# Interleaving VectorE's expert and gate products, and inverting attention's softmax sums in a compact layout

## The chip, the core and the metric

The kernel runs on one core of a Trainium2 chip. Its time is the device time of one execution in microseconds. Several runs are taken; the median of three is 2377.94 us (2376.03 to 2380.96). One further execution was profiled, and all durations of single instructions come from it.

The core has engines that each work through a queue of their own: PE (TensorE, matmuls), VectorE (DVE in the profile), ScalarE (ACT), GpSimd (POOL) and SyncE (SP, which here only issues DMAs). They wait for each other by semaphores.

## The reference

A layer norm feeds two branches, and the result is `x + A(xn) + B(xn)`, for 2048 tokens of width 512.

```python
# A: attention, 32 heads of width 16, one shared k and v
scores = jnp.einsum("bhqd,bkd->bhqk", q, k) * (Dh ** -0.5)
p = _softmax(scores, axis=-1)
o = jnp.einsum("bhqk,bkd->bhqd", p, v)
...
# B: 4096 experts by product keys, 32 heads, 2 experts of each head
s1 = jnp.einsum("nhd,ed->nhe", q1, k1)
s2 = jnp.einsum("nhd,ed->nhe", q2, k2)
...
g = _softmax(top_s, axis=-1)
ue = u[top_e]
ve = v[top_e]
act = _gelu(jnp.einsum("nd,nhkd->nhk", xf, ue))
out = jnp.einsum("nhk,nhk,nhkd->nd", g, act, ve)
```

So every token picks 64 experts: for each it takes the dot of its own row with the expert's row of `u`, puts a gelu and a gate on it, and adds that multiple of the expert's row of `v`.

## The kernel before

The tokens stand in four groups of 512. A start part computes the layer norm, k, v and q, and stores what is needed later in DRAM. Then one loop in hand-written order (`manual_schedule`: each engine runs its instructions in the order of the code) carries four kinds of work:

**Attention.** `att_steps` is one step of 256 and handles two of a unit's 16 key chunks; a unit is four heads of 512 query rows, 32 units in all. `scores` (L311) makes two score tiles per chunk on PE, and ScalarE takes their exp (L314) into a probability tile `pt`, of which there are five. `pv` (L325) multiplies the four tiles of the step before with v; v has columns of ones beside it, so that the sums of the softmax come out as sixteen equal rows below each head's output. After the last chunk `unit_tail` copies the result to `e` (L333), and eight DMAs on SP take it apart into `ot` (outputs) and `rsb` (sums, still sixteen equal rows). Two units make a pair; 20 steps after a pair's start `pair_tail` inverts `rsb` (L349) and multiplies (L351) into `on`. `block_out` multiplies four pairs with wo (L360) and adds the experts' part, through one tile `fin`.

**Expert scores.** A generator, `score_thread`, is advanced a fixed amount in each step, at its end (`fill`, `run_scores`). It makes the key scores on PE (L452) for chunks of four heads, and VectorE finds the best two of each (L462, L464); `batch` turns them into expert numbers `idx` and gates `gg`, ten buffers each. `SEQ` is the order of the chunks: group 0, four chunks of group 1, group 2 and its dense stage, the rest of group 1, group 3 and its dense stage.

**Gathered experts (groups 0 and 1).** The work is 512 slots; a slot is one expert of 128 tokens. `gather` (L732, GpSimd) fetches the rows of u and v into one of nine tiles. `dot` (L744) multiplies the u half with the token's row, into a junk tile of which there is one, and sums up; after four dots L748 and L750 make the argument of the gelu's tanh, which `tanh` (L755) takes on ScalarE. `add` (L766, L767 before the first of four, then L772) adds the weighted v half to the accumulator. A slot's gather can start when the add nine slots before is done.

**Dense experts (groups 2 and 3).** `dense` first forms all gates by one-hot products on VectorE (L611 to L614) and PE (L628). Then, for 32 blocks of 128 experts, PE makes the dots (L675), ScalarE their squares (L694), VectorE two products out of PSUM (L695 for `g`, L696 for `y`), ScalarE the tanh of `y` (L704), and VectorE three more products (`gate`, L699 to L701), the last of which reads what the two others wrote. PE multiplies by v (L655) and VectorE adds (L658). GpSimd splits the raw rows for the matmuls (L589).

The order on VectorE within a step is set by the main loop:

```python
            if d < half * 3 // 4:
                pos += 2.4 if dense_on[0] else 1.65
            ...
            dots(int(pos + 0.001))
            def mid():
                tanhs(before)
                run(ON_ACT)
                run(BEHIND)
                adds(4)
                gathers(4)
```

`pos` is the slot to which the dots have to come; after three quarters of the steps the rest is spread evenly. So a turn of VectorE is: the step's dots, then what `behind` put aside (the gate products), then up to four adds, and, at the end of the step, what the generator brings. `tanhs` and `ON_ACT` put the two kinds of tanh into ScalarE's queue, behind the step's first two exps. `store` puts DMAs aside until the start of the next step (`run(STORES)`).

Of the kernel before, what the change touches and what calls it, by code (L numbers as in the profile page):

```python
# [22 lines left out]
P = 128  # L23
S = 2048
D = 512
# [17 lines left out]
NIDX = 10  # L43
# [10 lines left out]
def tile_kernel(ctx, tc, x, wq, wkv, wo, wqT, kT, uv, ub, vb, out):  # L54
# [21 lines left out]
    d_m = dram.tile([2, H, S], F32, name="dm")  # L76
    d_part = [dram.tile([P, D], F32, name=f"dpart{t}") for t in range(NT)]
# [107 lines left out]
    def project_kv(g):  # L185
# [17 lines left out]
        sq = big.tile([16, 512], BF16, name="ksq", tag="junk", bufs=1)  # L203
# [9 lines left out]
    def project_q(g, wqs):  # L213
        pq = xtile("pqs")
        for r in range(KC):
            p = stile("pq")[:, 0, :]
            n = 0
            for k in range(KC):
                for a, b in TERMS:
                    nc.tensor.matmul(p, wqs[k][:, a, r * P:(r + 1) * P], XT[g][k][:, b, :],  # L220
                                     start=n == 0, stop=n == 11)
                    n += 1
            q = [start.tile([P, 512], F32R, name="qt", tag="qt", bufs=4) for _ in range(2)]
            nc.scalar.copy(q[0], p)
            nc.vector.tensor_tensor(out=q[1], in0=p, in1=q[0], op=OP.subtract)
            sq = big.tile([P, 512], BF16, name="qsq", tag="junk", bufs=1)
# [12 lines left out]
    def guard():  # L239

        mm = small.tile([P, 2], F32, name="mm")
# [5 lines left out]
        m2 = small.tile([1, 2], F32, name="m2")  # L247
        nc.vector.reduce_max(m2, p[:1, :2 * P].rearrange("p (a n) -> p a n", a=2), axis=AX.X)
        pr = small.tile([1, 1], F32, name="prd")
        nc.vector.tensor_mul(pr, m2[:, 0:1], m2[:, 1:2])  # L250
        fl = small.tile([1, 1], I32, name="flag")
# [5 lines left out]
    def true_maxima():  # L257
        ptile = lambda dt, shape: late[0].tile(list(shape), dt, name="mx", tag="pt", bufs=5)
# [48 lines left out]
    def scores(u, kc, i):  # L307
        p = stile("sc")
        for b in range(2):
            o = 64 * b  # L310
            nc.tensor.matmul(p[:, b, :], kaug[o:o + 64, kc * P:(kc + 1) * P], QA[u][o:o + 64, i, :],  # L311
                             start=True, stop=True)
        pt = late[0].tile([P, 2, 512], F32, name="pt", tag="pt", bufs=5)
        nc.scalar.activation(pt, p, AF.Exp, scale=SCALE)  # L314
        PT[u, kc, i] = pt
# [14 lines left out]
    def unit_tail(u):  # L330
# [4 lines left out]
        def spread():  # L335
            if half == 0:
                ot = late[0].tile([P, 512], F32, name="ot", tag="ot", bufs=1)
                rs = late[0].tile([P, 512], F32, name="rsb", tag="rsb", bufs=1)
                OT[pp], RB[pp] = ot, rs
            for j in range(4):  # L340
                o = slice(64 * half + 16 * j, 64 * half + 16 * j + 16)
                nc.sync.dma_start(OT[pp][o, :], e[32 * j:32 * j + 16, :])
                nc.sync.dma_start(RB[pp][o, :], e[32 * j + 16:32 * j + 32, :])

        store(spread)

    def pair_tail(pp):
        rs = RB.pop(pp)
        nc.vector.reciprocal(rs, rs)  # L349
        on = late[0].tile([P, 512], F32, name="on", tag="on", bufs=4)  # L350
        nc.vector.tensor_mul(on, OT.pop(pp), rs)  # L351
        ON[pp] = on

    DONE_A, DONE_B = {}, {}

    def block_out(qb, j):
# [5 lines left out]
        fin = late[0].tile([P, D], F32, name="fin", tag="fin", bufs=1)  # L362
        if t in DONE_B:
            nc.sync.dma_start(fin, d_part[t])
# [57 lines left out]
    def wp_read(n, ks=range(KC)):  # L422
        for k in ks:
# [4 lines left out]
    SEQ = ([(0, c) for c in range(NC)] + [(1, c) for c in range(4)] + [(2, c) for c in range(NC)]  # L428
           + [(1, c) for c in range(4, NC)] + [(3, c) for c in range(NC)])
# [127 lines left out]
    def dense(DG, after):  # L557

        flush()
        df1, df2, dgt = DT[:3]  # L560
        formed = [0]
# [107 lines left out]
        for b in range(NB):  # L669
# [24 lines left out]
            nc.scalar.activation(y, p, AF.Square, scale=C_CUB ** 0.5)  # L694
            stt(g, g, 1.0 / GS, p, op0=OP.mult, op1=OP.mult)  # L695
            stt(y, y, C_IN, p, op0=OP.add, op1=OP.mult)  # L696

            def gate(y=y, g=g, wd=wd):
                stt(wd[:, 0, :], y, 1.0, g, op0=OP.add, op1=OP.mult)  # L699
                stt(y, y, 1.0, g, op0=OP.add, op1=OP.mult)  # L700
                nc.vector.tensor_tensor(out=wd[:, 1, :], in0=y, in1=wd[:, 0, :], op=OP.subtract)  # L701
# [3 lines left out]
            behind(gate)  # L705
            held.append((wd, vs))
# [16 lines left out]
    UV, WT, ACTS, TH = {}, {}, {}, {}  # L723
# [13 lines left out]
    def dot(m):  # L737
# [5 lines left out]
        junk = big.tile([P, D], BF16, name="junk", tag="junk", bufs=1)  # L743
        nc.vector.tensor_tensor_reduce(junk, UV[m][:, :D], XN[TPH * ph + ti], scale=1.0, scalar=0.0,  # L744
                                       op0=OP.mult, op1=OP.add, accum_out=a[:, i:i + 1])
        if i == SB - 1:
# [4 lines left out]
            TH[n] = y  # L751

# [5 lines left out]
    def add(m):  # L758
        ph, c, ti, s = slots[m]
        n, i = divmod(m, SB)  # L760
        if i == 0:
            a, th = ACTS.pop(n), TH.pop(n)
            s0 = s
            ga = small.tile([P, SB], F32, name="ga", bufs=3)
            w = small.tile([P, SB], F32, name="w", bufs=3)
            nc.vector.tensor_mul(ga, a, G[ph, c, ti][:, s0:s0 + SB])  # L766
# [90 lines left out]
    def att_steps(d, mid, fill):  # L857
# [22 lines left out]
        if i >= 40 and (i - 40) % 32 == 0 and i - 40 < STEPS:  # L880
            pair_tail((i - 40) // 32)
# [53 lines left out]
    with tc.manual_schedule(engines={E_.PE, E_.Activation, E_.DVE, E_.Pool, E_.SP}):  # L935
# [3 lines left out]
        for d in range(half + 24):  # L939

            if d < half * 3 // 4:
                pos += 2.4 if dense_on[0] else 1.65
            else:
                pos += max(0.0, NSL - pos) / max(half - 4 - d, 1)
            before = d_next[0]
            dots(int(pos + 0.001))

            def mid():
                tanhs(before)
                run(ON_ACT)  # L950
                run(BEHIND)
                adds(4)
# [49 lines left out]
```

## Time and profile before

| | |
|---|---|
| median of three runs | 2377.94 us |
| the profiled execution, and the span of its instructions | 2381.03 us, 2379.1 us |
| granted clock of PE, mean | 0.909 |
| DMA: bytes moved, mean rate | 491.99 MB, 207 GB/s |
| ScalarE's exps (L314), busy | 1016.9 us |
| slot dots and adds (L744, L772), busy | 410.3 and 385.0 us |

A row of the groups view reads: line, engine, operation, output tile<-inputs, shapes, count, then busy time and mean of one in ns, then the engine's idle time just before these instructions, and what ended it. A row of the timeline reads: start and duration in us, engine, line, operation, tiles, count of merged instructions, and in brackets the idle time before and its releaser. A row of the stages view reads: stretch, its length, busy time and count of PE, PEld (weight loads), DVE, ACT and POOL, then the granted clock, the DMA engines' share and GB/s; limited to one line of the code, it has only the engines that the line uses. A row of the waits view reads: who waited, for whom, us in total, times, longest.

### The profile page before, as it was taken

What the parts mean: (1) busy time and instruction counts of PE and PEld (TensorE: products, weight loads), DVE (VectorE), ACT (ScalarE), POOL (GpSimd) and SP (SyncE); (2) the same over time, 40 slices, a digit from 0 to 9 for tenths busy, and PEclk for the clock granted to TensorE, in tenths of its full rate; (3) what the DMA queues carried; (4) which work ended last, traced back from release to release, by engine and by line L of the source; (5) the groups of instructions that cost most, each with busy time, mean ns of one, the idle gap of its engine ahead of it and who ended that gap; (6) DMA issues with size and microseconds to landing.
All of it is one profiled execution on the core that took longest, in us unless ns stands there. A gap on an engine that the chain in (4) does not pass through costs nothing.

```text
span 2379.1 us, 35223 instructions
## 1 busy us (share of the span) xinstructions
PE 2019.6 (85%) x10990; PEld 1064.9 (45%) x10990; DVE 1928.2 (81%) x6683; ACT 1274.4 (54%) x1702; POOL 767.9 (32%) x670
## 2 busy tenths in 40 slices
PE   5859899999987788888888899997777888888886
PEld 3534444545444344444444455544343444444442
DVE  5648788999997577999988689999786879899882
ACT  2335455555555565656565455554565555565652
POOL 2012222222231224544544322222124344445430
PEclk9979999999998779999899999999777898999897
DMA  5776666776564566766756876755467666666561
GB/s 196 259 251 205 220 220 244 263 247 224 189 206 127 156 170 208 232 190 203 233 190 220 286 254 224 258 188 173 123 178 227 207 204 197 206 219 213 195 200 65
DMA packets 236097, 491.99 MB, mean 207 GB/s; under 512 B 90736, under 2 KB 90736, under 8 KB 235904
## 3 DMA queue, kind: packets, MB, share of 16 engines
q0 software_dynamic: 73728, 268.47, 33.9%
q1 hardware_dynamic: 159504, 218.17, 28.6%
q10 hardware_dynamic: 2672, 3.05, 0.4%
q8 instruction: 88, 1.44, 0.2%
q14 instruction: 105, 0.86, 0.1%
HBM read 422.18 MB, written 58.20 MB: 202 GB/s over the span
## 4 chain that ended last, share of the span: by engine, by line
DVE 28%; PE 27%; issue 21%; POOL 9%; DMA 6%; ACT 2%; SPq 1%; POOLq 0%; DVEq 0%; ACTq 0%
PE pv L325 8%; PE psc L452 6%; DVE xa L772 6%; PE sc L311 6%; POOL g L732 5%; DVE i L464 5%; DVE junk L744 4%; POOL wk L589 4%; DVE m L462 3%; DMA g<-in_uv_dram,idx 2%; PE pwo L360 2%; ACT pt L314 2%; PE pout L655 2%; PE pact L675 1%; DVE rsb L349 1%
## 5 line engine op out<-in xcount | busy, mean ns | idle before, releaser
L314 ACT ACTIVATE pt<-sc 128x1024 f32<-128x1024 f32 x1024 | 1016.9, 1024 | 584.2 <-PE sc L311 474.8
L732 POOL DMA_INDIRECT g<-in_uv_dram,idx x512 | 584.9, 1142 | 1506.2 <-DVE xa L772 1295.0
L325 PE MATMUL pv<-pt,vaug 128*32 128x512 f32 x4096 | 540.8, 649 | 0.0
L311 PE MATMUL sc<-qa,kaug 64*128 64x512 f32 x2048 | 441.6, 492 | 57.2 <-ACT pt L314 44.5
L744 DVE CUSTOM_DVE_ANT_0 junk<-g,xa 128x512 bf16<-128x512 f32 x512 | 410.3, 801 | 56.3 <-DMA g<-in_uv_dram,idx 47.3
L772 DVE SCALAR_TENSOR_TENSOR xa<-g,w,xa 128x512 f32<-128x512 f32 x512 | 385.0, 752 | 18.5 <-DVE w L767 0.6
L452 PE MATMUL psc<-wk,xt 128*128 128x512 f32 x1536 | 386.6, 402 | 15.1 <-DMA xt<-dxt 4.1
L311 PEld LDWEIGHTS sc<-qa,kaug 64*128 64x128 f32 x2048 | 182.5, 194 | 442.8 <-ACT pt L314 292.9
L452 PEld LDWEIGHTS psc<-wk,xt 128*128 128x128 f32 x1536 | 280.8, 189 | 101.3 <-issue 21.4
L655 PE MATMUL pout<-wk,wd 128*128 128x512 f32 x768 | 224.1, 443 | 87.6 <-DVE gy L696 71.6
L675 PE MATMUL pact<-xt,wk 128*128 128x512 f32 x768 | 215.9, 430 | 33.3 <-DVE da L658 18.5
L325 PEld LDWEIGHTS pv<-pt,vaug 128*32 128x32 f32 x4096 | 113.1, 115 | 277.0 <-issue 275.5
L655 PEld LDWEIGHTS pout<-wk,wd 128*128 128x128 f32 x768 | 158.2, 213 | 139.7 <-DVE gy L696 82.9
L464 DVE FIND_INDEX8 i<-m,psc 128x8 uint32<-128x64 f32 x1024 | 206.3, 220 | 0.0
L675 PEld LDWEIGHTS pact<-xt,wk 128*128 128x128 f32 x768 | 152.1, 205 | 84.2 <-DVE da L658 22.6
L589 POOL TENSOR_TENSOR wk<-rw,wk 128x512 fp32r<-128x512 f32 x128 | 166.3, 1328 | 40.4 <-ACT wk L588 32.8
L462 DVE MAX8 m<-psc 128x8 f32<-128x64 f32 x1024 | 146.0, 213 | 40.1 <-PE psc L452 40.1
L628 PE MATMUL pg<-oh 128*128 128x32 f16 x1024 | 75.5, 247 | 56.8 <-DVE oh L614 56.8
L704 ACT ACTIVATE gy<-gy 128x512 f32<-128x512 f32 x64 | 40.3, 631 | 132.7 <-DVE gy L696 132.0
L628 PEld LDWEIGHTS <-oh 128*128 128x128 f16 x1024 | 70.9, 161 | 66.7 <-DVE oh L611 44.5
L588 ACT CAST wk<-rw 128x512 fp32r<-128x512 f32 x128 | 74.0, 629 | 35.7 <-PE pout L655 21.0
L658 DVE TENSOR_TENSOR da<-da,pout 128x512 f32<-128x512 f32 x128 | 82.2, 679 | 5.4 <-PE pout L655 5.4
(144 smaller groups left out, 1455.9 us busy)
## 6 DMA issues: line engine op xcount, KB each, us to landing
wk<-dw SPq DMA_DIRECT2D x96, 512.0 KB
wqt<-in_wqT_dram SPq DMA_DIRECT2D x32, 512.0 KB
dw<-wk SPq DMA_DIRECT2D x32, 512.0 KB
rw<-in_ub_dram SPq DMA_DIRECT2D x64, 256.0 KB
rw<-in_vb_dram SPq DMA_DIRECT2D x64, 256.0 KB
dg<-gst SPq DMA_DIRECT2D x32, 512.0 KB
gy<-dg SPq DMA_DIRECT2D x64, 256.0 KB
g<-in_uv_dram,idx POOLq DMA_INDIRECT x512
```

What stands on the lines that cost most here:

```text
L311: nc.tensor.matmul(p[:, b, :], kaug[o:o + 64, kc * P:(kc + 1) * P], QA[u][o:o + 64, i, :], start=True, stop=True)
L314: nc.scalar.activation(pt, p, AF.Exp, scale=SCALE)
L325: nc.tensor.matmul(PV[u][32 * j:32 * j + 32, :], vaug[:, kc, :], pt[:, b, :], start=kc == 0, stop=kc == 15)
L452: nc.tensor.matmul(p, XT[g][k][:, a, j * P:(j + 1) * P], WC[n_][k][:, bb, :], start=n == 0, stop=n == 11)
L462: nc.vector.max(m8[:, jb, s, :], p[:, s * E:(s + 1) * E])
L464: nc.vector.max_index(i8[:, jb, s, :], m8[:, jb, s, :], p[:, s * E:(s + 1) * E])
L589: nc.gpsimd.tensor_tensor(out=w[:, 1, :], in0=rw[:, i, :], in1=w[:, 0, :], op=OP.subtract)
L655: nc.tensor.matmul(p, wd[:, a, j * P:(j + 1) * P], vs[:, c, :], start=n == 0, stop=n == 5)
L675: nc.tensor.matmul(p, us[:, a, k * P:(k + 1) * P], XT[DG][k][:, c, :], start=n == 0, stop=n == 11)
L732: nc.gpsimd.indirect_dma_start(out=gt, out_offset=None, in_=uv, in_offset=bass.IndirectOffsetOnAxis(ap=IDX[ph, c, ti][:, s:s + 1], axis=0))
L744: nc.vector.tensor_tensor_reduce(junk, UV[m][:, :D], XN[TPH * ph + ti], scale=1.0, scalar=0.0, op0=OP.mult, op1=OP.add, accum_out=a[:, i:i ...
L772: nc.vector.scalar_tensor_tensor(acc, v, w[:, i:i + 1], acc, op0=OP.mult, op1=OP.add)
```

## The change

On VectorE a turn now alternates: one set-aside product group, one dot, one add, and again, until all three are used up. The gate is split in two groups: the two products, and the difference that reads them. The two products out of PSUM change places, `y` first. A dot writes its products over the u row that it has read, and the junk tile is gone (the start part's squares get tiles of their own). The product of dot and gate, `ga`, moves from `add` to `dot`. A step does as many adds as it has dots, two at least, while attention runs.

The sums of a pair (not of the last) go by another way: one row of each head is written to DRAM (`d_sum`), read back as 128 x 32, inverted there, written to DRAM (`d_inv`) and read back spread over sixteen rows each, into a tile that shares its place with `e`. This takes 4 to 14 key chunks after the pair's end, in five steps of code. There are six probability tiles in place of five, nine index buffers in place of ten. Slots per step are 1.75 in the score stages, 1.2 in the one-hot stages and 2.4 in the dense ones. `SEQ` takes two chunks of group 1 ahead of group 2 instead of four. At the end four `fin` tiles are loaded in one go into probability tiles.

```diff
@@
-NIDX = 10
+NIDX = 9
@@ project_kv, and likewise project_q
-        sq = big.tile([16, 512], BF16, name="ksq", tag="junk", bufs=1)
+        sq = start.tile([16, 512], BF16, name="ksq", tag="sq", bufs=2)
@@ scores
-        pt = late[0].tile([P, 2, 512], F32, name="pt", tag="pt", bufs=5)
+        pt = late[0].tile([P, 2, 512], F32, name="pt", tag="pt", bufs=6)
@@ unit_tail
+            if pp < 15:
+                nc.sync.dma_start(d_sum[pp, 4 * half:4 * half + 4, :],
+                                  e.rearrange("(j r) n -> j r n", r=32)[:, 16, :])
             for j in range(4):
                 o = slice(64 * half + 16 * j, 64 * half + 16 * j + 16)
+                if pp == 15:
+                    nc.sync.dma_start(RB[pp][o, :], e[32 * j + 16:32 * j + 32, :])
                 nc.sync.dma_start(OT[pp][o, :], e[32 * j:32 * j + 16, :])
-                nc.sync.dma_start(RB[pp][o, :], e[32 * j + 16:32 * j + 32, :])
...
+    def pair_load(pp):
+        rc = small.tile([P, 32], F32, name="rc", bufs=1)
+        nc.sync.dma_start(rc, d_sum[pp].rearrange("h n -> (h n)").rearrange("(p n) -> p n", n=32))
+        RC[pp] = rc
+
+    def pair_invert(pp):
+        rc = RC.pop(pp)
+        nc.vector.reciprocal(rc, rc)
+        store(lambda: nc.sync.dma_start(d_inv[pp].rearrange("h n -> (h n)").rearrange("(p n) -> p n", n=32), rc))
+
+    def pair_spread(pp):
+        rs = late[0].tile([P, 512], F32, name="rsb", tag="e", bufs=1)
+        RB[pp] = rs
+        nc.sync.dma_start(rs, d_inv[pp].rearrange("h n -> h () n").to_broadcast([8, 16, 512]))
 
     def pair_tail(pp):
         rs = RB.pop(pp)
-        nc.vector.reciprocal(rs, rs)
-        on = late[0].tile([P, 512], F32, name="on", tag="on", bufs=4)
-        nc.vector.tensor_mul(on, OT.pop(pp), rs)
+        ot = OT.pop(pp)
+        if pp == 15:
+            nc.vector.reciprocal(rs, rs)
+            on = ot
+        else:
+            on = late[0].tile([P, 512], F32, name="on", tag="on", bufs=4)
+        nc.vector.tensor_mul(on, ot, rs)
         ON[pp] = on
...
+    def load_fin():
+        for j in range(4):
+            if 12 + j in DONE_B:
+                pt = late[0].tile([P, 2, 512], F32, name="pt", tag="pt", bufs=6)
+                FIN[j] = pt[:, 0, :]
+                nc.sync.dma_start(FIN[j], d_part[12 + j])
@@
-    SEQ = ([(0, c) for c in range(NC)] + [(1, c) for c in range(4)] + [(2, c) for c in range(NC)]
-           + [(1, c) for c in range(4, NC)] + [(3, c) for c in range(NC)])
+    SEQ = ([(0, c) for c in range(NC)] + [(1, c) for c in range(2)] + [(2, c) for c in range(NC)]
+           + [(1, c) for c in range(2, NC)] + [(3, c) for c in range(NC)])
@@ dense
         df1, df2, dgt = DT[:3]
+        dense_on[0] = 2
...
             nc.scalar.activation(y, p, AF.Square, scale=C_CUB ** 0.5)
+            stt(y, y, C_IN, p, op0=OP.add, op1=OP.mult)
             stt(g, g, 1.0 / GS, p, op0=OP.mult, op1=OP.mult)
-            stt(y, y, C_IN, p, op0=OP.add, op1=OP.mult)
 
             def gate(y=y, g=g, wd=wd):
                 stt(wd[:, 0, :], y, 1.0, g, op0=OP.add, op1=OP.mult)
                 stt(y, y, 1.0, g, op0=OP.add, op1=OP.mult)
+
+            def rest(y=y, wd=wd):
                 nc.vector.tensor_tensor(out=wd[:, 1, :], in0=y, in1=wd[:, 0, :], op=OP.subtract)
                 formed[0] += 1
 
             on_act(lambda y=y: nc.scalar.activation(y, y, AF.Tanh))
             behind(gate)
+            behind(rest)
@@ dot
-        junk = big.tile([P, D], BF16, name="junk", tag="junk", bufs=1)
-        nc.vector.tensor_tensor_reduce(junk, UV[m][:, :D], XN[TPH * ph + ti], scale=1.0, scalar=0.0,
+        u = UV[m][:, :D]
+        nc.vector.tensor_tensor_reduce(u, u, XN[TPH * ph + ti], scale=1.0, scalar=0.0,
                                        op0=OP.mult, op1=OP.add, accum_out=a[:, i:i + 1])
...
+            ga = small.tile([P, SB], F32, name="ga", bufs=4)
+            nc.vector.tensor_mul(ga, a, G[ph, c, ti][:, s0:s0 + SB])
+            GA[n] = ga
@@ att_steps
-        if i >= 40 and (i - 40) % 32 == 0 and i - 40 < STEPS:
-            pair_tail((i - 40) // 32)
+        pp, r = divmod(i, 32)
+        if pp and pp < 16:
+            if r == 4:
+                pair_load(pp - 1)
+            if r == 6:
+                pair_invert(pp - 1)
+            if r == 10:
+                pair_spread(pp - 1)
+            if r == 14:
+                pair_tail(pp - 1)
+        if i == STEPS + 4:
+            load_fin()
+            pair_tail(15)
@@ the main loop
-                pos += 2.4 if dense_on[0] else 1.65
+                pos += (1.75, 2.4, 1.2)[dense_on[0]]
             else:
                 pos += max(0.0, NSL - pos) / max(half - 4 - d, 1)
-            before = d_next[0]
-            dots(int(pos + 0.001))
 
             def mid():
-                tanhs(before)
+
+                tanhs(d_next[0])
                 run(ON_ACT)
-                run(BEHIND)
-                adds(4)
+                rest = BEHIND[:]
+                BEHIND.clear()
+                todo = min(int(pos + 0.001), NSL) - d_next[0]
+                sums = min(a_ready[0] - a_next[0], max(todo, 2) if d < half else 4)
+                while rest or todo > 0 or sums > 0:
+                    if rest:
+                        rest.pop(0)()
+                    if todo > 0:
+                        dots(d_next[0] + 1)
+                        todo -= 1
+                    if sums > 0:
+                        adds(1)
+                        sums -= 1
                 gathers(4)
```

More of the change, by code (lines that the diff above doesn't have):

```diff
@@ L225, in project_q @@
             nc.vector.tensor_tensor(out=q[1], in0=p, in1=q[0], op=OP.subtract)
-            sq = big.tile([P, 512], BF16, name="qsq", tag="junk", bufs=1)
+            sq = start.tile([P, 512], BF16, name="qsq", tag="sq", bufs=2)
             nc.scalar.activation(sq, p, AF.Square)
@@ L361, in block_out @@
                              start=k == 0, stop=k == KC - 1)
-        fin = late[0].tile([P, D], F32, name="fin", tag="fin", bufs=1)
+        if qb == 3 and j in FIN:
+            fin = FIN[j]
+        else:
+            fin = late[0].tile([P, D], F32, name="fin", tag="fin", bufs=1)
         if t in DONE_B:
-            nc.sync.dma_start(fin, d_part[t])
+            if j not in FIN:
+                nc.sync.dma_start(fin, d_part[t])
             nc.vector.tensor_add(fin, fin, p)
```

28 lines of the change are left out of this document (16 added, 12 removed).

## The prediction

> **What bounds the kernel now.** First the page's busy shares, then the engines by stage. The stage bounds are mine: expert scores of groups 0 and 1 (160 to 713 us), one-hot gates (to 898), dense experts (to 1345), scores (to 1657), one-hot (to 1816), dense (to 2303), end.
>
> ```profile
> PE 2019.6 (85%) x10990; PEld 1064.9 (45%) x10990; DVE 1928.2 (81%) x6683; ACT 1274.4 (54%) x1702; POOL 767.9 (32%) x670
> ```
> ```profile
> 160.00:713.00 553.00, 510.36 (x2780) 263.10 (x2780) 475.05 (x2708) 295.80 (x356) 126.81 (x113) 0.96 0.66 226
> 713.00:898.00 185.00, 144.86 (x1043) 72.10 (x1044) 124.27 (x251) 104.35 (x163) 43.71 (x35) 0.78 0.55 154
> 898.00:1345.00 447.00, 378.31 (x1931) 205.95 (x1931) 396.59 (x700) 263.88 (x355) 210.80 (x178) 0.92 0.66 215
> 1345.00:1657.00 312.00, 294.98 (x1600) 157.47 (x1598) 280.32 (x1673) 167.78 (x198) 78.35 (x70) 0.99 0.65 225
> 1657.00:1816.00 159.00, 118.28 (x934) 60.23 (x934) 121.60 (x270) 91.69 (x150) 43.55 (x35) 0.75 0.64 175
> 1816.00:2303.00 487.00, 414.08 (x2044) 221.60 (x2044) 418.20 (x752) 276.55 (x371) 227.78 (x191) 0.91 0.63 203
> ```
>
> Columns: length, then PE, PEld, DVE, ACT, POOL busy, PE clock. In the score stages PE is busy 92 and 95%: PE sets the pace, VectorE (86 and 90%) close behind. In the dense stages VectorE leads (89 and 86%) over PE (85%). In the one-hot stages nobody is above 78%: a serial ring of VectorE, PE and ScalarE.
>
> An attention step is eight score matmuls, sixteen pv and some fill. Their counts by stage give the steps: 552/8 = 69, 160/8 = 20, 328/8 = 41, 136/8 = 17.
>
> ```profile
> 160.00:713.00 553.00, 115.12 (x552) 47.78 (x552) 0.96 0.66 226
> 713.00:898.00 185.00, 36.01 (x160) 15.03 (x160) 0.78 0.55 154
> 1345.00:1657.00 312.00, 68.37 (x328) 28.24 (x328) 0.99 0.65 225
> 1657.00:1816.00 159.00, 31.88 (x136) 13.04 (x136) 0.75 0.64 175
> ```
>
> One PE-paced step, in the timeline:
>
> ```profile
> 401.05 0.73 PE L311 MATMUL sc<-qa,kaug 64*128 64x512 f32 x4
> ...
> 402.88 1.02 ACT L314 ACTIVATE pt<-sc 128x1024 f32<-128x1024 f32 x1 [0.20 <-PE pv L325]
> 403.57 0.88 PE L311 MATMUL sc<-qa,kaug 64*128 64x512 f32 x4
> 403.95 0.19 PEld L311 LDWEIGHTS sc<-qa,kaug 64*128 64x128 f32 x2 [0.20 <-ACT pt L314]
> ...
> 408.01 0.73 PE L311 MATMUL sc<-qa,kaug 64*128 64x512 f32 x4
> ```
>
> 408.01 - 401.05 = 6.96 us is the floor of a step. The second exp waits 0.20 us for a probability buffer, and the second score group then takes 0.88 instead of 0.73 us.
>
> **The change part by part.**
>
> *Six probability buffers.* The wait for pv goes, and with it up to 0.88 - 0.73 = 0.15 us of a PE-paced step, nothing of others. 69 + 41 steps x 0.15 = 16.5; a few are not PE-paced: 15 us at most, 10 for the first stage and 5 for the second. Late next is the exp pair itself.
>
> *Dots in place, woven adds.* VectorE in the dense stage:
>
> ```profile
> 1011.60 0.68 DVE L744 CUSTOM_DVE_ANT_0 junk<-g,xa 128x512 bf16<-128x512 f32 x1
> ...
> 1012.32 0.69 DVE L744 CUSTOM_DVE_ANT_0 junk<-g,xa 128x512 bf16<-128x512 f32 x1
> ...
> 1013.33 0.68 DVE L744 CUSTOM_DVE_ANT_0 junk<-g,xa 128x512 bf16<-128x512 f32 x1
> 1013.94 0.08 DVE L744 DVE_READ_ACCUMULATOR2_ANT act<- 128x1 f32 x1
> 1013.94 0.69 DVE L699 SCALAR_TENSOR_TENSOR wd<-gy 128x512 fp32r<-128x512 f32 x1
> 1014.66 0.69 DVE L700 SCALAR_TENSOR_TENSOR gy<-gy 128x512 f32<-128x512 f32 x1
> 1015.39 0.69 DVE L701 TENSOR_TENSOR wd<-gy,wd 128x512 fp32r<-128x512 f32 x1
> ...
> 1021.58 3.11 DVE L772 SCALAR_TENSOR_TENSOR xa<-g,w,xa 128x512 f32<-128x512 f32 x4
> 1024.61 1.88 DVE L658 TENSOR_TENSOR da<-da,pout 128x512 f32<-128x512 f32 x3
> 1026.40 0.68 DVE L744 CUSTOM_DVE_ANT_0 junk<-g,xa 128x512 bf16<-128x512 f32 x1
> ```
>
> A dot followed by a dot, which writes the same junk tile, takes 0.72 us from start to start; followed by a gate product, which needs nothing of it, 0.61. Four adds, each reading the acc that the one before wrote, take 3.03/4 = 0.76; three sums into different tiles 1.79/3 = 0.60. So a need of the instruction just ahead costs 0.11 to 0.16 us. The weave puts another instruction between: an add falls to 0.60, saving 0.16. A dot saves 0.11 only where a dot followed it, about half: 0.05. Together 0.21 per slot. L701, moved behind a dot and an add, saves 0.73 - 0.61 = 0.12. Moving `ga` from add to dot changes no count. The bounds per slot are 0, if these gaps are not the dependence, and 0.27.
>
> The Trainium skill (VectorE: DVE Perf Modes, The DRAIN you can't avoid) says the opposite: a VectorE instruction flushes its pipe before the next starts, with or without a semaphore, so only fewer instructions help. By that the slot saves nothing and the sum below gives 2338. The 0.61 beside 0.72 above disagrees with it.
>
> *Compact inversion.* Fifteen of sixteen reciprocals shrink from 512 to 32 columns.
>
> ```profile
> L349 DVE RECIPROCAL rsb<-rsb 128x512 f32<-128x512 f32 x16 | 53.5, 3342 | 21.9 <-DMA rsb<-e 21.9
> ```
> ```profile
> L547 DVE RECIPROCAL gd<-den 128x16 f32<-128x16 f32 x16 | 4.1, 254 | 0.5
> ```
>
> The small one is nearest to the 16-column row: 0.25 us, so 3.1 saved each, one per 16 steps: 3 in the first dense stage, 4 in the second, 2 and 1 in the one-hot ones, 5 in the score ones. Bounds: nothing saved at the larger row's price, 3.1 at the smaller's.
>
> In its place come three transfers per pair. On SP 16 issues become 10 + 3:
>
> ```profile
> 2350.18 0.59 SPq L343 DMA_DIRECT2D rsb<-e  x1
> ...
> 2352.36 3.35 DVE L349 RECIPROCAL rsb<-rsb 128x512 f32<-128x512 f32 x1 [21.89 <-DMA rsb<-e]
> ```
>
> An issue is 0.59 us and lands 2.2 us after it begins. Load, inversion, spread and product are one or two steps apart (7 us and more), which hides each landing; without that cover VectorE would wait 2 x 2.2 us for each of 15 pairs, 66 us. Three new waits stand in SP's queue: the load and the spread wait for a DRAM write to land (2.2 us each), the store for VectorE's inversion. Behind them queue the loads of weights, gates and q, which are asked for one or two blocks before ScalarE and PE use them: I take zero, at most 2.2 x 30 = 66 us if every one were late. The spread sums share the tile of `e`; so ScalarE's copy of the next unit, and behind it two exps and PE's next pv, wait for the pair's product of one step before: zero in the forecast, at most about 1 us for 15.
>
> *Pacing.* One-hot steps do 1.2 slots for 1.65: 20 x 0.45 = 9 and 13 x 0.45 = 6 fewer (four of the 17 steps lie in the last quarter, where the rest is spread). A slot costs 0.72 + 0.76 = 1.5 us. They go to the score stages (1.75 for 1.65) and some 4 to the second dense stage. Scoring two instead of four chunks before the dense stage moves no total. Nine index buffers hold the chunks then alive by my count from the pacing.
>
> *Gates at the head.* Each VectorE turn now begins with the gate, whose tanh was covered by dots.
>
> ```profile
> 2289.54 0.68 DVE L696 SCALAR_TENSOR_TENSOR gy<-gy,pact 128x512 f32<-128x512 f32 x1
> ...
> 2290.25 0.64 ACT L704 ACTIVATE gy<-gy 128x512 f32<-128x512 f32 x1 [3.61 <-DVE gy L696]
> ```
>
> The tanh would be bare for about 0.7 us where L696 comes last. But the change swaps L695 and L696, so the tanh starts 0.60 earlier, beside the other product: I take 0.2 us x 64 gates (bounds 0 and 2: ScalarE's two exps stand ahead of it). Behind the gate on VectorE stand the turn's dots and adds, and behind these the gathers.
>
> *The end.* Four `fin` loads come early instead of one after each store.
>
> ```profile
> 2356.49 14.08 PE L360 MATMUL pwo<-wo_s,on 128*128 128x512 f32 x26 [8.55 <-DVE on L351]
> ...
> 2375.23 0.69 DVE L365 TENSOR_TENSOR fin<-fin,pwo 128x512 f32<-128x512 f32 x1 [4.81 <-DMA fin<-dpart]
> ```
>
> The last product is ready at 2370.6, the last add starts at 2375.2: 5 us. The startup's second square buffer: zero.
>
> *The sum.* The slots in the dense stages:
>
> ```profile
> L744 DVE CUSTOM_DVE_ANT_0 junk<-g,xa 128x512 bf16<-128x512 f32 x118 | 116.7, 989 | 12.9 <-DMA g<-in_uv_dram,idx 11.7
> ```
> ```profile
> L744 DVE CUSTOM_DVE_ANT_0 junk<-g,xa 128x512 bf16<-128x512 f32 x129 | 112.7, 873 | 22.1 <-DMA g<-in_uv_dram,idx 20.4
> ```
>
> First dense: 118 x 0.21 = 24.8, + 9.3 + 32 x 0.12 = 3.8, - 6.4 = 31. Second: 27 + 12.4 + 3.8 - 6.4 - 4 x 1.3 = 32. PE at 85% takes over part of the time, so two thirds: 21 + 21. One-hot: 13.5 + 5 + 6.2 = 25 and 9 + 5.5 + 3 = 17.5, half of it in waits of the ring: 12 + 9. Score stages: 10 + 5 of PE, and a quarter of VectorE's 20 each: 15 + 10. End 5. Sum 93 us. 2381 of the profiled execution (span 2379.1 and 1.9 around) less 93 is 2288; the median of the runs shown, 2377.94, lies 3 below that execution: 2285.
>
> **The rivals.**
>
> *The gaps stay.* If 0.72 and 0.76 are not the dependence, pacing, reciprocals, PE's 15 and the end are left. Dense: 9.3 - 6.4 and 12.4 - 6.4 - 5.2, two thirds: 2 + 1. One-hot: half of 19.7 and 12: 10 + 6. Score stages 9 + 7, since VectorE there gets more slots at the old price. End 5. Together 40 us, 2338. For it: L658 reads PSUM, L772 does not, so 0.60 may not be its price. Against: 0.61 and 0.72 are one instruction.
>
> *GpSimd lets go.* A dense dot means 0.99 and 0.87 us for a normal 0.68. Why:
>
> ```profile
> 1006.12 5.00 POOL L589 TENSOR_TENSOR wk<-rw,wk 128x512 fp32r<-128x512 f32 x4
> ```
> ```profile
> 1007.29 4.38 DVE L351 TENSOR_TENSOR on<-ot,rsb 128x512 f32<-128x512 f32 x1
> ```
>
> A product of two SBUF tensors ended when GpSimd's splits did. With gathers trickling, the splits may fall beside the PSUM sums instead: 118 x 0.31 + 129 x 0.19 = 61, two thirds 41: 2243, or 2215 if the small products gain alike. The Trainium skill (SBUF — State Buffer, SBUF: two separate sides) calls this port an exclusive lock held for the whole instruction; the 4.38 agrees. Against: the turns hold the same products as before.
>
> *Slower: waits at the head of the turn.* ScalarE does two exps before the expert's tanh; in the one-hot stages `w` already waits behind dots:
>
> ```profile
> L767 DVE SCALAR_TENSOR_TENSOR w<-gth,ga 128x4 f32<-128x4 f32 x8 | 1.3, 163 | 28.5 <-ACT gth L755 28.5
> ```
>
> 28.5/8 = 3.6 us. If 64 gates and 128 `w`, covered by at most one dot, wait 0.75 us more, that is 144 against 93: 2378 + 51 = 2429. It decides from 93/192 = 0.5 us. Against: in the dense stages VectorE arrives late, and `w` there follows the gate's tanh.
>
> *Slower: gathers too late.* Adds are spread, so gathers go out later: by my count of the pacing, slots whose dot comes one step after the gather rise from 47 to 158.
>
> ```profile
> DVE junk L744 <- DMA g<-in_uv_dram,idx: 47.3, 33, 5.7
> ```
>
> Threefold waits add 95 to 110 and eat all: 2378 + 10 = 2388.
>
> **How the numbers follow.** Forecast 0.55; gaps stay 0.14; GpSimd 0.10; head waits 0.12; gathers 0.09, a third of it still just faster. Faster 0.55 + 0.14 + 0.10 + 0.03 = 0.82, same 0.02, slower 0.16; 0.2% (5 us) is what these runs can tell. The range goes from 2205, 10 us under the far end of the GpSimd case, to 2380, where the gains are just eaten; the slower cases beyond it and a little below are the two tenths left out. The forecast's own is 2240 to 2320.
>
> **What would show it.** Right: VectorE busy falls by about 53.5 - 8 us of reciprocals and 512 x 0.15; dots and adds alternate 0.61 apart; floor steps last 6.81; VectorE's idle before the gate stays under 15 us; dense stages near 425 and 465 us. Wrong: idle before `w` or the gate above 100 us, waits for gathers above 140, or dots that still follow 0.72 apart.

## The result and the profile after

The changed kernel takes 2257.14 us (median of 4 runs, 2251.6 to 2261.62) against 2379.45 beside it: a ratio of 0.9486 [0.9457, 0.9514], 122 us less. The forecast was 2285, its own range 2240 to 2320, the whole range 2205 to 2380. The profiled execution took 2254.1 us with a span of 2252.2.

First the page's busy shares, then the engines by stage (columns as before; bounds are mine: first scores, one-hot, dense, scores, one-hot, dense, end).

```profile
PE 1961.7 (87%) x10990; PEld 1036.4 (46%) x10990; DVE 1804.8 (80%) x6683; ACT 1253.4 (56%) x1704; POOL 730.7 (32%) x670
```
```profile
169.00:654.00 485.00, 446.77 (x2516) 231.12 (x2516) 421.65 (x2452) 261.84 (x323) 113.00 (x106) 0.98 0.70 235
654.00:820.00 166.00, 142.62 (x1064) 69.50 (x1065) 105.66 (x229) 104.49 (x165) 37.90 (x29) 0.84 0.59 156
820.00:1230.00 410.00, 362.69 (x1947) 200.00 (x1945) 365.55 (x708) 260.90 (x355) 202.15 (x179) 0.95 0.74 234
1230.00:1590.00 360.00, 338.51 (x1826) 178.77 (x1826) 310.12 (x1951) 188.08 (x228) 86.79 (x82) 0.96 0.67 225
1590.00:1729.00 139.00, 119.14 (x938) 61.08 (x939) 104.90 (x239) 89.29 (x148) 36.68 (x30) 0.76 0.71 186
1729.00:2189.00 460.00, 402.66 (x2095) 214.50 (x2093) 387.09 (x785) 280.84 (x383) 221.21 (x198) 0.94 0.72 227
```

VectorE's busy time fell by 123 us. In the dense stages it no longer stands clear of PE: 89 and 84% against PE's 88 and 88%. The granted clock of PE is 0.925 for 0.909, but the pv matmuls, the largest group on PE, take 648 ns on average where they took 649, so the gain is not that PE's work itself became faster. Because two chunks are now scored after the dense stage, the stages don't hold the same steps in both kernels. Measured from the first score matmul of a step to that of a later one, with the steps counted:

| stage | before, us (steps) | after, us (steps) | forecast gain |
|---|---|---|---|
| scores 1 | 553.5 (69) | 484.9 (62) | 15 |
| one-hot 1 | 184.6 (20) | 166.9 (21) | 12 |
| dense 1 | 467.5 (51) | 409.9 (49) | 21 |
| scores 2 | 291.9 (39) | 359.4 (47) | 10 |
| one-hot 2 | 158.6 (17) | 139.1 (17) | 9 |
| dense 2 | 497.3 (53) | 460.7 (53) | 21 |
| end, to the last add | 73.7 | 70.4 | 5 |

A dense step went from 9.17 to 8.37 us in the first and from 9.38 to 8.69 in the second: at equal steps some 41 and 37 us. The one-hot stages gave about 26 and 19.5. The two score stages together need 844 us for 109 steps where 845 went for 108: 9 us. The start, before the first step, is 9 us longer in this profile (158.0 for 149.2) and 9 to 11 longer in every run below. By then eight adds are done and seventeen gathers issued, where it was two adds and ten gathers, so this is not the time of the same work, and I draw nothing from it.

A PE-paced step, in the timeline of after:

```profile
422.36 0.73 PE L313 MATMUL sc<-qa,kaug 64*128 64x512 f32 x4
422.96 1.94 ACT L316 ACTIVATE pt<-sc 128x1024 f32<-128x1024 f32 x2 [5.08 <-PE sc L313]
...
424.88 0.73 PE L313 MATMUL sc<-qa,kaug 64*128 64x512 f32 x4
...
429.17 0.73 PE L313 MATMUL sc<-qa,kaug 64*128 64x512 f32 x4
```

429.17 - 422.36 = 6.81 us. Both score groups take 0.73, and the two exps run without a gap.

A woven turn in the dense stage, on VectorE and then on GpSimd:

```profile
963.73 3.03 DVE L742 SCALAR_TENSOR_TENSOR wd<-gy 128x512 fp32r<-128x512 f32 x1
966.80 0.69 DVE L743 SCALAR_TENSOR_TENSOR gy<-gy 128x512 f32<-128x512 f32 x1
967.41 0.68 DVE L790 CUSTOM_DVE_ANT_0 g<-g,xa 128x512 f32<-128x512 f32 x1
968.02 0.08 DVE L790 DVE_READ_ACCUMULATOR2_ANT act<- 128x1 f32 x1
968.02 0.75 DVE L819 SCALAR_TENSOR_TENSOR xa<-g,w,xa 128x512 f32<-128x512 f32 x1
968.68 0.68 DVE L746 TENSOR_TENSOR wd<-gy,wd 128x512 fp32r<-128x512 f32 x1
969.28 0.68 DVE L790 CUSTOM_DVE_ANT_0 g<-g,xa 128x512 f32<-128x512 f32 x1
```
```profile
963.66 2.54 POOL L632 TENSOR_TENSOR wk<-rw,wk 128x512 fp32r<-128x512 f32 x2
```

From the dot to the add behind it are 0.61 us, from the add on 0.66. Over the whole trace a dot is followed after 0.61 us (median of 227 that an add follows), an add by another kind of instruction after 0.67 (180 dots), and an add by an add after 0.785, which happens 53 times where it happened 382 times before. The gate, L742, began 0.07 us after GpSimd's two splits and took 3.03 us: it ended 0.56 us after them. The dots were held in that way before; now the gate stands there. Groups of after, with the inversion's:

```profile
L790 DVE CUSTOM_DVE_ANT_0 g<-g,xa 128x512 f32<-128x512 f32 x512 | 380.4, 744 | 46.9 <-DMA g<-in_uv_dram,idx 46.8
L742 DVE SCALAR_TENSOR_TENSOR wd<-gy 128x512 fp32r<-128x512 f32 x64 | 93.8, 1465 | 26.4 <-ACT gy L749 24.7
...
L365 DVE RECIPROCAL rc<-rc 128x32 f32<-128x32 f32 x15 | 5.1, 341 | 1.8 <-DMA rc<-dsum 1.8
```

and its waits on VectorE:

```profile
DVE w L814 <- ACT gth L805: 70.0, 26, 8.6
DVE g L790 <- DMA g<-in_uv_dram,idx: 46.8, 36, 5.0
...
DVE wd L742 <- ACT gy L749: 24.7, 17, 3.2
```

Of the kernel before, the waits of `w` and the idle time of the gate (by groups), not shown yet:

```profile
DVE w L767 <- ACT gth L755: 70.1, 25, 6.7
```
```profile
L699 DVE SCALAR_TENSOR_TENSOR wd<-gy 128x512 fp32r<-128x512 f32 x64 | 50.8, 793 | 5.8 <-ACT gy L704 5.7
```

So the waits for gathers and those before `w` are what they were (47 and 70 us), and the wait before the gate has grown from 5.7 to 24.7.

### The profile page after: what moved, and what is told of

Same layout as the page of the kernel before. It is cut to its first block, busy times and chain, and to the rows that moved or that the text cites. A ratio compares the mean times of both kernels' runs of the same rounds, so it can differ in the third digit from the quotient of the medians.

```text
span 2252.2 us, 34914 instructions
## 1 busy us (share of the span) xinstructions
PE 1961.7 (87%) x10990; PEld 1036.4 (46%) x10990; DVE 1804.8 (80%) x6683; ACT 1253.4 (56%) x1704; POOL 730.7 (32%) x670
## 5 line engine op out<-in xcount | busy, mean ns | idle before, releaser
L316 ACT ACTIVATE pt<-sc 128x1024 f32<-128x1024 f32 x1024 | 991.0, 1024 | 571.5 <-PE sc L313 568.9
L778 POOL DMA_INDIRECT g<-in_uv_dram,idx x512 | 552.2, 1078 | 1440.1 <-DVE xa L819 1227.7
L313 PE MATMUL sc<-qa,kaug 64*128 64x512 f32 x2048 | 401.6, 464 | 62.7 <-ACT pt L316 45.4
L790 DVE CUSTOM_DVE_ANT_0 g<-g,xa 128x512 f32<-128x512 f32 x512 | 380.4, 744 | 46.9 <-DMA g<-in_uv_dram,idx 46.8
L313 PEld LDWEIGHTS sc<-qa,kaug 64*128 64x128 f32 x2048 | 163.1, 191 | 403.5 <-ACT pt L316 254.7
L698 PE MATMUL pout<-wk,wd 128*128 128x512 f32 x768 | 213.6, 428 | 59.7 <-DVE gy L739 41.3
L718 PE MATMUL pact<-xt,wk 128*128 128x512 f32 x768 | 211.9, 424 | 28.0 <-DVE da L701 21.1
L698 PEld LDWEIGHTS pout<-wk,wd 128*128 128x128 f32 x768 | 151.2, 203 | 112.9 <-DVE gy L739 49.7
L718 PEld LDWEIGHTS pact<-xt,wk 128*128 128x128 f32 x768 | 150.5, 203 | 83.6 <-DVE da L701 25.5
L632 POOL TENSOR_TENSOR wk<-rw,wk 128x512 fp32r<-128x512 f32 x128 | 161.8, 1290 | 20.1 <-ACT wk L631 19.0
L742 DVE SCALAR_TENSOR_TENSOR wd<-gy 128x512 fp32r<-128x512 f32 x64 | 93.8, 1465 | 26.4 <-ACT gy L749 24.7
L671 PEld LDWEIGHTS <-oh 128*128 128x128 f16 x1024 | 70.4, 160 | 37.3 <-DVE oh L654 15.4
L654 DVE TENSOR_TENSOR oh<-oh 128x2048 f16<-128x2048 f16 x64 | 78.0, 1219 | 10.5 <-POOL oh L646 8.0
```

What stands on the lines that cost most here:

```text
L632: nc.gpsimd.tensor_tensor(out=w[:, 1, :], in0=rw[:, i, :], in1=w[:, 0, :], op=OP.subtract)
L698: nc.tensor.matmul(p, wd[:, a, j * P:(j + 1) * P], vs[:, c, :], start=n == 0, stop=n == 5)
L718: nc.tensor.matmul(p, us[:, a, k * P:(k + 1) * P], XT[DG][k][:, c, :], start=n == 0, stop=n == 11)
L778: nc.gpsimd.indirect_dma_start(out=gt, out_offset=None, in_=uv, in_offset=bass.IndirectOffsetOnAxis(ap=IDX[ph, c, ti][:, s:s + 1], axis=0))
L790: nc.vector.tensor_tensor_reduce(u, u, XN[TPH * ph + ti], scale=1.0, scalar=0.0, op0=OP.mult, op1=OP.add, accum_out=a[:, i:i + 1])
```

## The experiments

All ratios are to the kernel before, with a 95% interval; the change itself is 0.9486. Edits are to the changed kernel, except in "The weave on the kernel before".

**The order inside a turn.** Three kernels do the same products, tile for tile. The first puts them back into blocks: dots, what is behind, adds.

```
-                while rest or todo > 0 or sums > 0:
-                    ...
+                dots(d_next[0] + todo)
+                for fn in rest:
+                    fn()
+                adds(sums)
```

> The changed kernel, but a turn of VectorE is again all dots, then all gate products, then all adds; how many of each a step does is as in the change. Spacing theory (the gain is the 0.11 to 0.12 us that VectorE loses between two instructions of which the second needs the first): two or three adds stand side by side again, some 270 gaps of 0.12 us come back (32 us on VectorE), two thirds of it in the time: 2275 to 2285, ratio to the kernel before about 0.958. Evenness theory (the gain is that dots and adds are spread evenly over the steps): nothing of that is undone, 2255 to 2262, 0.949. Head-of-turn theory (the weave itself costs, because gate and w are no longer covered by dots): a little faster than the change, 2235 to 2250, 0.942.

Measured: 2393.74 us, 1.0049 [1.0028, 1.0069]: a little slower than before the change, and far outside all three expectations. The waits view, and a turn of the second dense stage on VectorE and GpSimd:

```profile
DVE g L790 <- DMA g<-in_uv_dram,idx: 198.3, 109, 6.3
```
```profile
2012.39 1.53 DVE L819 SCALAR_TENSOR_TENSOR xa<-g,w,xa 128x512 f32<-128x512 f32 x2
...
2015.03 0.69 DVE L790 CUSTOM_DVE_ANT_0 g<-g,xa 128x512 f32<-128x512 f32 x1
...
2018.36 0.69 DVE L790 CUSTOM_DVE_ANT_0 g<-g,xa 128x512 f32<-128x512 f32 x1 [2.63 <-DMA g<-in_uv_dram,idx]
...
2021.08 0.69 DVE L790 CUSTOM_DVE_ANT_0 g<-g,xa 128x512 f32<-128x512 f32 x1 [2.02 <-DMA g<-in_uv_dram,idx]
```
```profile
2013.40 1.35 POOL L778 DMA_INDIRECT g<-in_uv_dram,idx  x1 [4.63 <-DVE xa L819]
2015.06 1.47 POOL L778 DMA_INDIRECT g<-in_uv_dram,idx  x1 [0.30 <-issue]
```

The adds come last, their gathers are issued at 2013.4 and 2015.1, and the dots that need just these rows stand in the next turn and wait 2.6 and 2.0 us for them. A gather lands 5.3 us after its issue (median, page of after). This is the fourth rival's mechanism: adds that are spread evenly, with the dots ahead of them, cost 151 us of waits. What stops it is the weave, by which a turn's last dots stand behind its adds.

The undo on the other side leaves the adds uneven too, as before the change: dots, the rest, then up to four adds.

```
+                dots(int(pos + 0.001))
+                run(BEHIND)
+                adds(4)
```

> The changed kernel with the whole turn as in the kernel before: all dots, all gate products, up to four adds. The run with even adds but dots first came out at 2394, with VectorE waiting 198 us for gathers (47 in the change). Gather theory (even adds let the gathers out later, and only a dot that stands behind the adds of its turn gives them time): with four adds at once the waits fall back to about 50 us, and what is left is the spacing, some 330 adds and the gate at 0.12 us, 45 us on VectorE: 2285 to 2300, 0.964. If dots ahead of the gate cost by themselves: waits stay above 120 us, 2350 or more.

Measured: 2323.21, 0.9758 [0.9727, 0.9789]: more than expected. So weaving and even adds together, with the gate at the head of the turn that comes with them, are worth 66 us.

```profile
DVE w L814 <- ACT gth L805: 85.7, 24, 8.5
...
DVE g L790 <- DMA g<-in_uv_dram,idx: 49.7, 37, 5.1
```

Gather waits are as in after, as the gather theory said; the time is 23 us above its range. By the spacing, 381 adds follow an add at 0.788 here: 328 more than in after at 0.12 are 39 us, and 64 gates' second product 7. Another 31 us are time in which products stood still beside GpSimd's splits: summed over the trace as the excess of each product over its group's median, 126 us here and 95 in after (119 before). 46 + 31 = 77. The two profiled executions, to which these figures belong, lie 79 us apart (2333.2 and 2254.1), the medians 66. And 195 dots follow a dot, 0.61 apart, where 193 stood 0.726 apart before: the inputs are the same, but the output is no longer a shared bf16 tile. The run with the junk tile, below, shows that the sharing is what counts. That settles the rival of the gaps. By the rule of the Trainium skill that the prediction weighed (VectorE: DVE Perf Modes, The DRAIN you can't avoid) the same number of instructions would take the same time; 0.726 and 0.61 disagree with it for these products. The same section of the Trainium skill also says that an instruction that is not held starts earlier, which the prediction left out; a dot of 0.68 us whose successor starts after 0.61 agrees with that.

Weaving without evenness:

```
-                sums = min(a_ready[0] - a_next[0], max(todo, 2) if d < half else 4)
+                sums = min(a_ready[0] - a_next[0], 4)
```

> The changed kernel, but a step does up to four adds as soon as a group of four is ready, in place of as many as it has dots. Spacing theory: two of four adds stand side by side, 256 gaps of 0.12 us come back, 31 us on VectorE, two thirds in the time: 2275 to 2280, 0.958. Evenness theory: heavy and light steps come back, 9 us or more in each dense step with four adds; most of the 70 us that the dense stages gave goes: 2300 or more, 0.967. If neither counts: 2257.

Measured: 2282.02, 0.9595 [0.9561, 0.963]. Gather waits are nearly gone:

```profile
DVE g L790 <- DMA g<-in_uv_dram,idx: 7.3, 4, 5.3
```

but 242 adds follow an add again (189 x 0.12 = 23 us) and 123 us are spent beside splits (after: 95). 40 us of waits are saved and some 50 lost; the two profiled executions lie 15 us apart, the medians 25: neither account is exact. Evenness is what lets the weave reach every slot; alone it is worse than nothing, by the first run.

**The weave on the kernel before.** In-place dots, the split of the gate, the mid loop with even adds; pacing, inversion, five buffers, chunk order and end as before.

```
-        nc.vector.tensor_tensor_reduce(junk, UV[m][:, :D], XN[TPH * ph + ti], scale=1.0, scalar=0.0,
+        u = UV[m][:, :D]
+        nc.vector.tensor_tensor_reduce(u, u, XN[TPH * ph + ti], scale=1.0, scalar=0.0,
...
+                while rest or todo > 0 or sums > 0:
+                    ...
```

> The kernel before with the weave, the split gate, the even adds and the dots in place, and nothing else (five probability buffers, old inversion, old pacing, g before y). Spacing and evenness theories: about half of the change, 2310 to 2330, 0.975. Head-of-turn theory: with g before y the tanh is bare at the head, 64 x 0.6 us on VectorE: 2345 to 2360, 0.988. If the gain came from pacing, inversion and buffers: 2370 or more.

Measured: 2323.76, 0.9768 [0.9742, 0.9795]: 55 us, with two waits larger than in after.

```profile
DVE g L747 <- DMA g<-in_uv_dram,idx: 64.5, 46, 6.1
...
DVE wd L699 <- ACT gy L706: 34.1, 29, 3.6
```

**Five probability buffers.** `tag="pt", bufs=5` at all three places.

> The changed kernel with five probability buffers. By the prediction's step each PE-paced step gets 0.14 to 0.15 us longer (6.81 to 6.95 us), some 100 to 150 steps: 15 to 21 us, 2272 to 2278, 0.956. Rival: ScalarE's wait is taken up elsewhere (its tanh comes later too, and VectorE's gate with it): 25 us or more, 0.960.

Measured: 2286.95, 0.96 [0.9561, 0.9639]: 30 us by the medians, 27 by the ratios, twice the forecast. The floor step is 6.95 again, and ScalarE waits 83 us for pv to free a buffer, 221 times, where after has no such wait among its longer ones. By stages: scores +9 and +2, one-hot +8 and +4, dense +4 and +1, the rest in start and end.

**A junk tile for the dots**, with five buffers to make room:

```
+        junk = big.tile([P, D], BF16, name="junk", tag="junk", bufs=1)
```

> The changed kernel with dots that write into one junk tile again, and five probability buffers to make room; to be compared with the run of five buffers. In the trace of the change only 9 of 512 dots are followed by a dot, so the junk tile should cost nothing once dots and adds alternate: same as the five-buffer run within 5 us. If writing the junk tile costs by itself (0.11 us per dot), 30 to 55 us more.

Measured: 2281.33, 0.9569 [0.955, 0.9589], not to be told from the run above. In its trace 227 dots are followed by an add after 0.61 us, and nine by another dot after 0.727: the junk tile costs only where the next instruction writes it too. Once adds stand between, writing in place earns nothing.

**The old inversion**, with five buffers: sixteen reciprocals of 512 columns, no round trip on SP.

> The changed kernel with the old inversion of sixteen equal rows (3.34 us on VectorE per pair, eight DMAs per unit) and five probability buffers. By the prediction's terms, against the five-buffer run: two thirds of 21.7 us in the dense stages, half of 9.3, a quarter of 15: about 23 us more. If VectorE's saving is hidden in PE-paced stages: 10 or less. If the DMA round trip had a price: faster than the five-buffer run.

Measured: 2295.87, 0.9636 [0.9614, 0.9659]: by the ratios 9 and 16 us over the two runs above. Its interval overlaps that of the first, which differs in nothing else, and not that of the second, which has the junk tile too. So a gain of the compact inversion is likely rather than shown, and it is below the 23 us in the sum.

**The old pacing.**

```
-                pos += (1.75, 2.4, 1.2)[dense_on[0]]
+                pos += (1.65, 2.4, 1.65)[dense_on[0]]
```

> The changed kernel with 1.65 slots in the score and in the one-hot steps; 2.4 and the rest as in the change. By the prediction's terms the one-hot stages get 15 slots back, at 0.61 + 0.67 us and half of it in waits: 10 us, the score stages lose 7, the last dense stage 3 or 4: 2262 to 2268, 0.951. Ring theory (in the one-hot stages a step with a w waits for a ring of three engines, and fewer groups mean fewer such steps): 15 groups' waits of 3.5 us return in part, 20 us or more.

Measured: 2240.95, 0.9413 [0.9394, 0.9432]: 16 us faster than the change, where both theories expected it slower. By stages: scores -3.5 and -10, one-hot +9.5 and +2.7, dense -12.8 and -4.2. By the dots in the trace, the one-hot stages do 14 slots more than in after (33 and 31 for 24 and 26), the score stages ten fewer, the first dense stage the same 117, the second four fewer.

**The two products ahead of the tanh, swapped back** (`g` before `y`).

> The changed kernel with g before y again. By the prediction's step the tanh starts 0.6 us later and the gate, first in its turn, stands bare for it: 64 x 0.6 = 38 us on VectorE, two thirds in the time: 2275 to 2285, 0.958. Rival: 27 of 64 gates stand still for GpSimd's splits at that place anyway (46 us), so most of it is hidden: 2257 to 2265, 0.950.

Measured: 2258.3, 0.9499 [0.9464, 0.9535]: no difference. The wait before the gate does grow, from 24.7 to

```profile
DVE wd L742 <- ACT gy L749: 34.3, 33, 3.0
```

**The gate behind the turn's first dot and add.**

```
+                lead = 1
                 while rest or todo > 0 or sums > 0:
-                    if rest:
+                    if rest and not lead:
...
+                    lead = 0
```

> The changed kernel, but each turn begins with one dot and one add, and the gate comes after them. Head-of-turn theory: the 25 us that the gate waits for its tanh go, and a third of what w adds: 2237 to 2247, 0.942. Lock theory: what stands first waits for GpSimd's splits; the 46 us move from the gate to the first dot, and only the tanh's 25 us can go, less what PE then waits for the later gate: 2247 to 2260, 0.948.

Measured: 2234.15, 0.939 [0.9355, 0.9424]: 23 us faster than the change.

```profile
L790 DVE CUSTOM_DVE_ANT_0 g<-g,xa 128x512 f32<-128x512 f32 x512 | 428.4, 838 | 46.7 <-DMA g<-in_uv_dram,idx 46.5
...
L742 DVE SCALAR_TENSOR_TENSOR wd<-gy 128x512 fp32r<-128x512 f32 x64 | 43.8, 684 | 2.9 <-ACT gy L749 2.9
```

The wait before the gate falls by 22 us, which is the size of the gain; by stages 14.5 us of it lie in the dense stages, where the gates are, and 7 in the second score stage, which this wait does not explain. The gate is back at 684 ns, but the dots went from 744 to 838: the stretch beside the splits only changed hands (95 us in all before this edit, 99 after).

**No splits on GpSimd.** The low parts of the split weights are filled with zeros.

```
-                    nc.gpsimd.tensor_tensor(out=w[:, 1, :], in0=rw[:, i, :], in1=w[:, 0, :], op=OP.subtract)
+                    nc.gpsimd.memset(w[:, 1, :].bitcast(F32), 0.0)
```

> The changed kernel, but GpSimd writes zeros where it computed the low parts of the dense experts' rows: that correction is left out of the result, and no GpSimd instruction reads two SBUF tensors. Lock theory (VectorE's products of two SBUF tensors stand still while GpSimd's splits run; excess of dots, gates and small products over their usual duration: 95 us in the change): the excess goes, dense stages shorter by half to two thirds, 45 to 65 us, 2195 to 2212, 0.926. If the excess only stands in for other waits: 2245 or more.

Measured: 2193.72, 0.9212 [0.9193, 0.9231]: 63 us under the change.

```profile
L790 DVE CUSTOM_DVE_ANT_0 g<-g,xa 128x512 f32<-128x512 f32 x512 | 351.1, 687 | 69.6 <-DMA g<-in_uv_dram,idx 68.6 <-issue 0.6
...
L742 DVE SCALAR_TENSOR_TENSOR wd<-gy 128x512 fp32r<-128x512 f32 x64 | 43.9, 686 | 41.0 <-ACT gy L749 39.4 <-ACT gth L805 0.8
```

Dots and gates are at their own 687 and 686 ns, the excess is 2 us for 95. Two thirds of it reach the time; against the rest stand 22 us more of gather waits and 15 more before the gate. The fill is also shorter on GpSimd than the product (542 ns for 1290), but gathers did not get earlier by it, and PE's expert dots (L718) had waited only 2.1 us for a split in after; so the gain is that VectorE is not held. By stages the dense ones are 40 and 28 us shorter, the others hardly change. By this run 63 us is about what keeping GpSimd's products out of VectorE's way could still bring.

**Old pacing and late gate together.**

> The run with 1.65 slots in score and one-hot steps (2241 us), with the gate after the first dot and add. If both count, 2241 less what the late gate gives: 2225 to 2235, 0.937. If the late gate gives nothing: 2241.

Measured: 2220.45, 0.9343 [0.9307, 0.9379], 37 us under the change, where 16 and 23 add to 39: a version faster than both kernels.

## Why the prediction was right, and where its terms were off

Direction and cause hold, and the time lies in the range; the gain is 122 us where 93 were forecast. The weave carried the change, the floor step is 6.81 us, and VectorE's busy time fell by 123 us where the working gives 45.5 + 77 = 122. That last agreement is partly luck, as the terms show. In the dense stages VectorE no longer stands clear of PE, but they still hang on it: in the run without splits, where GpSimd doesn't hold it, they are 69 us shorter.

The gains in the sum, put together over the stages, beside what the runs say:

| term | in the sum | measured by undoing it |
|---|---|---|
| slots in place and woven, L701 | 54 | 66, net of the next row |
| gate at the head | -8.5 | -23 |
| six buffers | 15 | 27 to 30 |
| compact inversion | 23 | 9 to 16 |
| pacing | +5 | -16 |
| end | 5 | 3 (stage table) |

The prediction does not split VectorE's 20 us in each score stage. Its rival without the slots' saving has 16 us there in place of 25, so the table gives the slots 9 of them and pacing -3. The 66 come from a run that keeps the dots in place and takes the gate off the head, so they stand beside at most 54 - 8.5 = 45.5.

*Dots in place, woven adds.* The mechanism is shown from both sides (66 us by undoing, 55 by doing it on the kernel before). The saving of an add was mis-sized: 0.60 was taken from L658, a sum that reads PSUM, and an instruction that does not need the add just ahead starts 0.67 after it. The 0.76 of four adds was an average of three needed gaps of 0.787 and one free one of 0.667. A slot saves 0.12 us, 329 x 0.12 + 193 x 0.114 = 61 us over the 512, not 0.21 and 107. This was made up by the shares. "Two thirds" in the dense stages and a half in the one-hot ones were too low: at equal steps they gave 41, 37, 26 and 19.5 instead of 21, 21, 12 and 9. Part of that is not spacing: in after VectorE stands 31 us less beside the splits than with blocked turns and uneven adds. This goes with the even adds and not with the weave: by the same sum the blocked turn with even adds has some 100 us, about as after (95), and the woven one with uneven adds 123.

*Six probability buffers.* 0.15 us of a floor step is right, and the score stages lost 11 us without it. The other part, 8 and 4 us in the one-hot stages and 5 in the dense ones, was set at nothing. The step that failed is "nothing of others". In the dense stages 26 of 102 steps of after are floor steps too, which covers 4 of the 5 us. That the one-hot stages gain because a free buffer shortens their ring of VectorE, PE and ScalarE is argued, not shown.

*Compact inversion.* 0.341 us for 32 columns, so 3.0 us saved where 3.1 was taken. Of the 23 us, 9 to 16 reached the time. SP's new waits were put at zero in the time, and at most 2.2 us each. Those of the stores are longer: ten of the fifteen stores wait for VectorE's inversion, up to 27 us (waits view of SP's DMA queue):

```profile
SPq L366 <- DVE rc L365: 113.2, 10, 27.1
```

Whether this took the other half wasn't tried.

*Pacing* failed in sign. The one-hot stages gain 12 us, where 11 stood in the sum, but the score stages, whose VectorE was read at 86 and 90%, were given the slots at a price of about 3 us: they lose 13.5, for ten slots. That the dense stages lose 17 with the same rate is measured and not explained: the first has the same 49 steps and 117 slots in both runs and is 12.8 us longer in after.

*Gates at the head.* 0.2 us x 64 = 13 was expected, under 15 us of idle time, and 24.7 came. The swap of L695 and L696, on which the 0.2 rested, moves the wait by 10 us and the time by nothing. A turn that begins with a dot and an add loses 22 of the 24.7.

*The rivals.* The gaps were the dependence. GpSimd lets go in part, with the even adds: 119 to 95 us. Head waits are there, 19 us more before the gate and none more before `w`: 0.1 us a wait where 0.5 was the point of decision. Gathers too late is real, 151 us with blocked turns, and was wrongly judged by counting slots alone: the place of a turn's last dots among its adds decides.

*What stays open.* The single undoings give 66 + 28 + 12 + 3 - 16 = 93 of the 122 us. The rest lies in what was not undone alone, the chunk order, or in how the parts act together: in-place dots, for one, save 22 us of spacing in a blocked turn and nothing in a woven one.

## What to carry to other kernels

Where an in-order engine does many like instructions, put another kind between two that need each other, and take the price from the same instruction in both places, not from a similar one. Spread producers and consumers together: spreading the releases of buffers alone made 109 of 512 dots wait for their rows here, and cost more than the change brought. Work that is moved out of a slack stage is not free in a stage where the engine is at 86 to 90%; undo each part of a change alone, since here two of its parts cost 37 us that the others hid.

## What the runs showed of the hardware

A product of two SBUF tensors on VectorE doesn't share with GpSimd's tensor products, it waits for them: 3.03 us beside two splits of 2.54 together. Moving the dots out of the way moved the wait to the gate, and moving the gate moved it back (95 and 99 us); only taking the splits away removed it. The dependence of one VectorE instruction on the one ahead costs 0.11 to 0.12 us at 512 columns, for the dot (0.726 to 0.612) and for the add (0.787 to 0.667) alike; a dot's shared output tile alone is enough for it (0.727 between two dots into the junk tile, 0.61 from such a dot to an add).
